# Four small edits to the order of work in a retention + two-MLP kernel: key scaling, weight sums, one held-back product, last stores

## The chip, the cores and the metric

The kernel runs on one core of a Trainium2 chip. The metric is the device time of one execution in microseconds (us). Before the change the median of three runs is 852.21 us (852.18 to 854.21).

## What is computed

Inputs are q, k and v (4 batches, 8 heads, 576 positions, 64 channels) and four weight matrices. In numpy terms:

```python
ret = scale * (q @ k.T) * Dmat          # Dmat: gamma ** distance below the diagonal, 0 above
x = (ret @ v)                           # 2304 tokens x 512
x = softplus(x @ w_in) @ w_out          # first MLP, 512 -> 2048 -> 512
out = (h * sigmoid(1.702 * h)) @ w2_out # second MLP, h = x @ w2_in
```

## The kernel before

Every factor of a large matrix product is split into a high and a low part (suffix h and l in the names), and a product is three matmuls: high by high, low by high, high by low. ACT casts the high part (`hi`, line 92) and DVE subtracts it to get the low part (`lo`, line 98). PE therefore has a long list of matmuls, and ACT and DVE prepare operands for it.

**Stages.** The tokens are cut into five blocks: the first 512 of each batch, and a short block "t" (256 columns) of the last 64 positions of all four batches. The order is batch 0, 1, 2, then "t", then batch 3 (line 297). Retention of batch 0 runs alone at the start (`first_batch`, line 556). Then the first MLP runs over the five blocks (`run_first`, line 213). Each block has 16 items f = 0 to 15: `mm1` makes 128 hidden features (tile ph, 12 matmuls), ACT applies softplus (tile g), `split` makes gh and gl, and `mm2` of the item two places back adds its share to the block's output (tile y, 12 matmuls). Then the second MLP runs (`run_second`, line 971) with a Strassen-like scheme of seven half-size products, so that its weights need sums and differences of their quarters.

**Work beside the first MLP.** While PE works on items, `side()` (line 685) is called four times an item. Each call adds a rate to two accumulators and advances two generators by one step for each whole unit:

- `side_gen` is the retention of the next batch (`batch`, line 538). A batch has eight pairs of heads-and-halves, and one pair takes three steps: `scale_pair` (line 364: ACT multiplies the pair's keys in place by decays, two instructions at line 373), then the pair's matmuls (`quad_step`, lines 463 and 502, into tile ps_so), then DVE's reading of that result (lines 510 to 533) and the load of the pair three places on (`load_pair`, line 353, DMA at line 356, on SP's queue, three buffers). A quad step also finishes the pair before it. Its first 16 matmuls use unscaled keys, the next need the scaled ones.
- `conv` is first the conversion of the first MLP's weights from 64-bit words (`convert_first`, line 113: ACT line 132, DVE lines 104, 105 and 110, ACT `hi`, DVE `lo`, tiles wa and w), then that of the second MLP's weights (`convert`), then the weight sums of the second MLP (`sums_steps`, line 746: four steps a unit, tiles sum and sum_halves). The sums run during block "t" at 0.66 step a call and during the last block at 0.7.

At a block's start, `pre` (line 1206) emits `split_block` (line 324): four ACT casts (tile xh) and four DVE subtractions (xl), each 128x512, and the block's first `mm1` reads them. Each engine executes its own instructions in the order in which they were emitted.

**Between the MLPs.** The first MLP's last three items still owe 36 products y (`pending`). The first two items of the second MLP (i = 0 and 1) work them off, 18 each, in five portions that stand ahead of places where PE must wait for ACT or DVE (`parts`, line 1034, taken by `fill`, line 1041): ahead of products 2 and 1, of product 6, of product 7, of products 4 and 5, and of product 3. All results of an item lie in halves X and Y of one PSUM bank (tile ph, line 1052).

**The end.** The second MLP's block "t" comes last (`second_layer_t`, line 919). It ends with two results y[0] and y[1], each one PSUM bank of 512 columns; y[0] is complete six matmuls before y[1]. `done_t` (line 1172) copies each to SBUF and stores it with two DMAs.

Of the kernel before, what the change touches and what calls it, by code (L numbers as in the profile page):

```python
# [16 lines left out]
T = 512  # L17
# [8 lines left out]
N2 = 256  # L26
# [7 lines left out]
def kernel(  # L34
# [36 lines left out]
    nc = tc.nc  # L71
# [4 lines left out]
    NF = w1_in.shape[0]  # L76
    KD = DM // P
    TAIL = S - T
# [13 lines left out]
    def hi(eng, dst, src):  # L92
        if eng == "a":
            nc.scalar.copy(dst, src)  # L94
        else:
            nc.vector.tensor_copy(dst, src)
# [197 lines left out]
    with tc.manual_schedule():  # L294
# [34 lines left out]
        def xf_tile():  # L329
            return xp.tile([P, KD, T], F32, tag="xf", name="xf")  # L330

        with ExitStack() as consts, ExitStack() as right, ExitStack() as second:
# [20 lines left out]
            def load_pair(i, tile_of=None, end_of=None):  # L353
                b, c, p = pairs[i]
                t = tile_of or ap.tile([P, KQV], F32, tag="raw", name="raw", bufs=RB)
                nc.sync.dma_start(out=t, in_=kqv[b, c, p])
                e = end_of
                if c and e is None:
                    e = ap.tile([P, ENDS], F32, tag="end", name="end", bufs=2)
                    nc.sync.dma_start(out=e, in_=ends[b, :, p])  # L360
                v = t[:, 2 * C0:].rearrange("p (t s d) -> p t s d", t=2, s=2)
                loaded[i] = t[:, 0:C0], t[:, C0:2 * C0], v[:, :, 0, :], v[:, :, 1, :], e

            def scale_pair(i, engines="aa", only="ap"):
                p, x = pairs[i][2], loaded[i][2]
                for h in range(2):
                    y, d = x[:, :, halves[h]], (sdec if i < 2 * NPAIR else sdec64)[:, 2 * p + h:2 * p + h + 1]
                    if engines[h] not in only:
                        continue
                    if engines[h] == "p":  # L370
                        nc.gpsimd.tensor_scalar(out=y, in0=y, scalar1=d, scalar2=None, op0=ALU.mult)
                    else:
                        nc.scalar.mul(y, y, d)
# [164 lines left out]
            def batch(b):  # L538

                xf[b] = xf_tile()  # L540
                i0, i1 = 2 * NPAIR * b, 2 * NPAIR * (b + 1)
                if b == 1:
                    for i in range(i0, i0 + RB):
                        load_pair(i)
                    yield
                for i in range(i0, i1 + 1):
                    if i < i1:
                        scale_pair(i)
                    yield
                    out_i = i - 1 if i > i0 else None  # L550
                    yield from quad_step(out_i, i if i < i1 else None)
                    if out_i is not None and out_i + RB < len(pairs):
                        load_pair(out_i + RB)
                    yield
# [77 lines left out]
            for _ in range(WARM):  # L632
# [3 lines left out]
                out=mask[:, 0:2, :].rearrange("p u j -> p (u j)"), in_=mask[:, 0:2, :].rearrange("p u j -> p (u j)"),  # L636
# [45 lines left out]
            conv = {"g": w1_gen, "acc": 0.0, "rate": 1.0}  # L682
# [236 lines left out]
            def second_layer_t(i):  # L919

                k, j = items[i]
                if j == 0:
                    sums_y[k] = [ps_y.tile([P, T], F32, tag="y", name="y") for _ in range(2)]
                for o in range(2):
                    gh, gl = g_operand(i, o)
                    for t in range(2):
                        c = slice(t * P, (t + 1) * P)
                        for n in range(2):
                            wh, wl = weight(i, "out", f"{o + 1}{n + 1}")
                            for z, (l, r) in enumerate(((gh, wh), (gl, wh), (gh, wl))):  # L930
                                seven([(l[:, c], r)], sums_y[k][t][:, n * N2:(n + 1) * N2],
                                      j == 0 and o == n == z == 0)
                                yield
                gs.pop(i)
# [36 lines left out]
            def run_second(pending):  # L971
# [52 lines left out]
                for i in range(n_items + 2):  # L1024
# [6 lines left out]
                    wino, post = cur is not None and not cur_t, prv is not None and not prv_t  # L1031

                    if i < 2:
                        more, parts = pending, ((4, 5, 3, 3, 3), (4, 5, 3, 3, 99))[i]
                    elif items[i - 2][0] == "t":
                        more, parts = second_layer_t(i - 2), (5, 3, 4, 4, 99)
                    else:
                        more, parts = second_layer(i - 2), (7, 10, 6, 7, 99)
                    parts = iter(parts)
# [14 lines left out]
                    if prv is not None:  # L1054
                        old = cs.pop(prv)
                        g = old["g"]
                        a = xp.tile([P, KD, T], F32R, tag="x8", name="ga", bufs=2)
                        a = a.rearrange("p (h k) (c n) -> p h (k c) n", h=2, c=2)
                        b = {}
                        gs[prv] = {"a": (a, ["11", "c3", "12", "22"] if post else [0, 1]), "b": b}  # L1060
                        if post:
# [4 lines left out]
                            c = {"c1": g[:, 4], "c2": g[:, 5], "c3": g[:, 1], "c4": g[:, 6]}  # L1066
# [104 lines left out]

            def done_t(e, y):
                yb = tp.tile([P, T], F32, tag="yb", name="yb", bufs=3)
                hi("v" if e % 2 else "a", yb, y)
                for j in range(2):
                    t0 = (2 * e + j) * S + T
                    nc.sync.dma_start(out=out[t0:t0 + TAIL, :], in_=yb[j * TAIL:(j + 1) * TAIL])

            n_full = NP * (len(order2) - 1)

# [25 lines left out]
            def pre(key, n, f):  # L1206
                i = order.index(key)
                if f == 0:
                    for _ in side_gen["g"]:
                        pass  # L1210
                    if i:
                        split_block(key, 1, xt if key == "t" else xf[key])
                        if turning:
                            turning.clear()
                            next(w2_gen, None)
                    if i + 1 < B:
                        side_gen["g"] = batch(i + 1)
                    else:
                        side_gen["g"] = iter(())
                    if key == "t":  # L1220
                        for _ in w2_gen:
                            pass
                        right.close()
                        cp = right.enter_context(tc.tile_pool(name="cp", bufs=2, side="right"))
                        sums_gen["g"] = sums_steps(cp)
                        conv.update(g=sums_gen["g"], rate=0.66)
                    if i + 1 == len(order):
                        conv["rate"] = 0.7
                        x2_load(order2[0])
                if i == 0:  # L1230
                    for n in range(0 if f else -1, 1):
                        w1_load(2 * (f + n) + 10, 2 * (f + n) + 11)
                    w1_need(f, 0)
                    w1_need(f - 2, 1)
                    counts[:] = STEPS[f] if f < len(STEPS) else ()
                    side_gen["rate"] = 0.62 if f >= 4 else 0.0
                    if f == NF - 2:
                        w2_read(0)
                        w2_read(1)
                    if f == NF - 1:  # L1240
                        for _ in w1_gen:
                            pass
                        next(w2_gen)
                        conv.update(g=w2_gen, acc=0.0, rate=1.0)
                elif i + 2 < len(order):
                    side_gen.update(acc=0.0 if f < 2 else side_gen["acc"], rate=0.52 if f else 0.0)
                    conv.update(acc=0.0, rate=1.0 if f or i == 2 else 0.0)
                if i < 2 and f == NF - 1:
                    turning.append(f)
                if i + 1 == len(order) and f >= 11:  # L1250
                    if f == 11:
                        for _ in sums_gen["g"]:
                            pass
                        right.close()
                        pool2["x"] = right.enter_context(tc.tile_pool(name="x2", bufs=1, side="right"))
                        consts.close()
                        pool2["g"] = second.enter_context(tc.tile_pool(name="g2", bufs=1))
                    if f == 12:
                        first_q.update(x_quarters(order2[0]))
                        for op in x_sums(order2[0], first_q):  # L1260
                            op()
                    if f >= 13:
                        names = [("21", "11"), ("c2", "c3"), ("c1", "c4", "22")][f - 13]
                        for late in [x_split(order2[0], nm, first_q[nm]) for nm in names]:
                            late()
# [83 lines left out]
```

## Time and profile before

| | |
|---|---|
| median of three runs | 852.21 us |
| the profiled execution | 852.78 us, of which the span from first to last instruction is 851.0 us |
| TensorE matmul (PE) busy | 834.7 us, 98% of the span |
| VectorE (DVE) busy | 568.7 us, 67% |
| ScalarE (ACT) busy | 405.3 us, 48% |
| mean granted TensorE clock | 0.997 of full speed |
| DMA | 217.70 MB, mean 256 GB/s |

PE rows are matmuls, PEld rows weight loads, and SPq rows DMA issues on SyncE's queue. In a timeline row the columns are start, duration, engine, line, operation, tiles written and read, shape and count; a bracket at the end is the idle time just before, with what ended it. The duration of a merged row (x12, say) runs from its first start to its last end. Matmul ends are modelled and overlap the next start: a 512-column matmul starts 0.227 us after the one before at full clock.

### The profile page before, as it was taken

The numbers are of one execution on the slowest core, as the hardware profiler recorded it, in microseconds if no ns is written. First come the engines' busy times: TensorE is split into PE (matmuls) and PEld (weight loads), VectorE is DVE, ScalarE is ACT, GpSimd is POOL, SyncE is SP. The second block draws the span as 40 slices with busy tenths as digits, with TensorE's granted clock in tenths as the row PEclk, the third lists the DMA queues.
The fourth block names the chain that finished last, engine by engine and source line by source line (L and its number), as shares of the span: only waits on it lengthen the run. The fifth ranks groups of instructions, "written<-read, shape, count | busy, mean of one in ns | idle before, by whom it ended". The sixth has DMA issues, their size and how long they took to land.

```text
span 851.0 us, 17585 instructions
## 1 busy us (share of the span) xinstructions
PE 834.7 (98%) x7115; PEld 751.4 (88%) x7115; DVE 568.7 (67%) x1158; ACT 405.3 (48%) x811; POOL 95.0 (11%) x178
## 2 busy tenths in 40 slices
PE   8989999999999999999999999999999999999997
PEld 5778888888888888997888899999999999999997
DVE  3998996666576764677434577787778777866621
ACT  4665545334453434455334555554555555554321
POOL 3200000211122111000000000100121011001000
PEclk9999999999999999999999999999999999999999
DMA  9966424898788874799996686977788779776611
GB/s 341 407 257 210 138 75 157 250 296 261 238 253 282 280 220 156 272 365 336 418 383 213 226 288 238 340 283 273 248 309 306 255 272 334 272 257 231 209 56 25
DMA packets 64481, 217.70 MB, mean 256 GB/s; under 512 B 6416, under 2 KB 21520, under 8 KB 52112
## 3 DMA queue, kind: packets, MB, share of 16 engines
q0 software_dynamic: 20704, 116.40, 39.8%
q1 hardware_dynamic: 43696, 100.17, 33.0%
q8 instruction: 56, 0.92, 0.4%
q14 instruction: 25, 0.20, 0.1%
HBM read 157.83 MB, written 58.72 MB: 254 GB/s over the span
## 4 chain that ended last, share of the span: by engine, by line
PE 85%; DVE 6%; DMA 4%; ACT 2%; issue 1%; SPq 0%; DVEq 0%; ACTq 0%
PE ph L878 20%; PE y L211 20%; PE ph L211 20%; PE m L878 18%; PE ps_so L463 3%; PE y L878 3%; DMA w_kqv<-kqv 1%; PE ps_so L502 1%; DMA odec<-outdecay 1%; DMA sums_in<-sum_halves 1%; DMA sums_out<-sum_halves 1%; DVE sum_halves L99 1%; DVE gl L99 0%; DMA whole<-whole_in 0%; DVE yb L950 0%
## 5 line engine op out<-in xcount | busy, mean ns | idle before, releaser
L211 PE MATMUL y<-gh,w 128*128 128x512 f32 (+1 forms) x640 | 197.3, 372 | 0.0
L211 PE MATMUL ph<-xh,w 128*128 128x512 f32 (+1 forms) x640 | 183.2, 371 | 2.3 <-ACT xh L94 2.3
L211 PEld LDWEIGHTS y<-gh,w 128*128 128x128 f32 x640 | 117.4, 189 | 21.0 <-issue 0.2
L211 PEld LDWEIGHTS ph<-xh,w 128*128 128x128 f32 x640 | 115.0, 189 | 23.0 <-ACT xh L94 2.9
L211 PE MATMUL y<-gl,w 128*128 128x512 f32 (+1 forms) x320 | 118.0, 369 | 0.0
L211 PE MATMUL ph<-xl,w 128*128 128x512 f32 (+1 forms) x320 | 118.0, 369 | 0.0
L878 PE MATMUL m<-w,ga 128*128 128x256 f32 x768 | 117.2, 282 | 0.5 <-DVE yb L950 0.5
L878 PE MATMUL ph<-xo_c,w 128*128 128x256 f32 x768 | 108.3, 283 | 0.0
L260 ACT ACTIVATE g<-ph 128x512 f32<-128x512 f32 (+1 forms) x80 | 44.2, 553 | 133.8 <-PE ph L211 131.1
L878 PE MATMUL ph<-xo,w 128*128 128x256 f32 x768 | 105.4, 282 | 0.5 <-DVE ho L1144 0.5
L99 DVE TENSOR_TENSOR gl<-g,gh 128x512 fp32r<-128x512 f32 (+1 forms) x80 | 50.8, 636 | 80.8 <-ACT gh L94 80.7
L878 PEld LDWEIGHTS m<-w,ga 128*128 128x128 f32 x768 | 102.8, 190 | 1.1 <-PE ph L878 1.1
L878 PEld LDWEIGHTS ph<-xo_c,w 128*128 128x128 f32 x768 | 97.9, 188 | 1.4 <-DVE he L1106 0.6
L878 PEld LDWEIGHTS ph<-xo,w 128*128 128x128 f32 x768 | 97.6, 189 | 1.5 <-DVE ho L1144 1.4
L878 PE MATMUL m<-w,gb 128*128 128x256 f32 x576 | 89.7, 282 | 0.0
L878 PEld LDWEIGHTS m<-w,gb 128*128 128x128 f32 x576 | 78.0, 191 | 0.0
L211 PEld LDWEIGHTS ph<-xl,w 128*128 128x128 f32 x320 | 60.3, 189 | 10.8 <-DVE xl L99 0.6
L211 PEld LDWEIGHTS y<-gl,w 128*128 128x128 f32 x320 | 60.5, 189 | 9.2
L99 DVE TENSOR_TENSOR ga<-g,ga 128x512 fp32r<-128x512 f32 x72 | 47.0, 685 | 9.1 <-ACT ga L94 9.1
L94 ACT CAST ga<-g 128x512 fp32r<-128x512 f32 x72 | 44.7, 621 | 15.3 <-PE y L878 7.9
L94 ACT CAST gh<-g 128x512 fp32r<-128x512 f32 (+1 forms) x80 | 46.3, 578 | 2.4
L99 DVE TENSOR_TENSOR gb<-g,gb 128x256 fp32r<-128x256 f32 x96 | 37.0, 419 | 13.8 <-ACT gb L94 13.8
(146 smaller groups left out, 1062.3 us busy)
## 6 DMA issues: line engine op xcount, KB each, us to landing
w<-sums_in POOLq DMA_DIRECT2D x32, 1024.0 KB, 5.5
w<-sums_out POOLq DMA_DIRECT2D x32, 1024.0 KB, 7.4
raw<-kqv SPq DMA_DIRECT2D x24, 512.0 KB, 4.7
w<-kept POOLq DMA_DIRECT2D x12, 1024.0 KB, 8.4
w_raw<-w_in SPq DMA_DIRECT2D x16, 512.0 KB, 9.6
w_raw<-w_out SPq DMA_DIRECT2D x16, 512.0 KB, 9.9
raw<-w_in POOLq DMA_DIRECT2D x16, 512.0 KB, 5.5
raw<-w_out POOLq DMA_DIRECT2D x16, 512.0 KB, 5.5
```

Source lines behind the costliest of these rows:

```text
L94: nc.scalar.copy(dst, src)
L99: nc.vector.tensor_tensor(out=dst, in0=src, in1=f32(h), op=ALU.subtract)
L211: nc.tensor.matmul(out_ap, l, r, start=first and i == 0, stop=last and i == k - 1)
L260: nc.scalar.activation(g, ph, AF.Softplus)
L463: nc.tensor.matmul(z[halves[half], t, at:at + D], l[halves[row]], rhs[halves[row]], start=(t, half) not in seen, stop=True, skip_group_che ...
L502: nc.tensor.matmul(z[n:n + D // 2, t, to:to + D], s[halves[h], m:m + D // 2], x[halves[h]], start=False, stop=True, skip_group_check=True)
L878: nc.tensor.matmul(out_ap, l, r, start=clear, stop=True, skip_group_check=True)
```

## The change

`batch` scales the first pair ahead of its loop, and from then on pair i+1 in the same step as pair i's matmuls, just ahead of them; the step that held only the scaling is now empty. `parts` of items 0 and 1 move one of the 18 products from the second portion to the last. The conversion rate is set to 0 at the last item of block "t", and for the last block it is 0.75 and not 0.7. `done_t` copies both results with DVE, the second one in two halves of 256 columns, and issues one store of each result on SP's queue and the other on ACT's.

```diff
@@ batch
+                scale_pair(i0)
                 for i in range(i0, i1 + 1):
-                    if i < i1:
-                        scale_pair(i)
                     yield
                     out_i = i - 1 if i > i0 else None
+                    if i + 1 < i1:
+                        scale_pair(i + 1)
                     yield from quad_step(out_i, i if i < i1 else None)
@@ run_second
-                        more, parts = pending, ((4, 5, 3, 3, 3), (4, 5, 3, 3, 99))[i]
+                        more, parts = pending, ((4, 4, 3, 3, 4), (4, 4, 3, 3, 99))[i]
@@ done_t
-                hi("v" if e % 2 else "a", yb, y)
-                for j in range(2):
+                for n in range(1 + e):
+                    c = slice(n * N2, (n + 1) * N2) if e else slice(0, T)
+                    hi("v", yb[:, c], y[:, c])
+                for j, queue in enumerate((nc.sync, nc.scalar)):
                     t0 = (2 * e + j) * S + T
-                    nc.sync.dma_start(out=out[t0:t0 + TAIL, :], in_=yb[j * TAIL:(j + 1) * TAIL])
+                    queue.dma_start(out=out[t0:t0 + TAIL, :], in_=yb[j * TAIL:(j + 1) * TAIL])
@@ pre
-                        conv["rate"] = 0.7
+                        conv["rate"] = 0.75
@@ pre
+                if key == "t" and f == NF - 1:
+                    conv["rate"] = 0.0
```

## Rows read from the trace of the kernel before

**Rows 1.** The profile page, busy time of each engine over the span.

```profile
PE 834.7 (98%) x7115; PEld 751.4 (88%) x7115; DVE 568.7 (67%) x1158; ACT 405.3 (48%) x811; POOL 95.0 (11%) x178
```

**Rows 2.** Waits of PE: us in total, times, longest.

```profile
PE ps_so L463 <- ACT raw L373: 2.4, 1, 2.4
PE ph L211 <- ACT xh L94: 2.3, 2, 1.7
```

**Rows 3.** Busy time by stretch, just after the longest wait of PE.

```profile
63.66:66.00 2.34, 2.34 (x56) 2.00 (x57) 2.34 (x3) 2.09 (x4) 0.00 (x0) 0.52 0.00 0
```

**Rows 4.** Timeline, ACT and PE around the second pair of batch 1.

```profile
53.77 1.15 ACT L132 ACTIVATE wa<-w_raw 128x1024 f32<-128x1024 f32 x1 [1.35 <-DVE w L99]
...
60.84 0.46 PE L463 MATMUL ps_so<-raw 64*64 64x64 f32 x16
...
62.25 1.04 ACT L94 CAST w<-wa 128x1024 fp32r<-128x1024 f32 x1 [3.89 <-DVE wa L110]
...
63.21 0.69 ACT L373 ACTIVATE raw<-raw,dec 128x128 f32<-128x128 f32 x2
```

**Rows 5.** The chain that ended last, in order of time: start, us, what.

```profile
69.57 2.72 PE ph L211 x12
...
82.35 1.08 PE ps_so L463 x56
...
83.78 2.95 PE ph L211 x12
...
89.45 1.36 PE ph L211 x6
...
272.13 1.08 PE ps_so L463 x56
```

**Rows 6.** Timeline, DVE: low parts of two weight pairs.

```profile
64.00 1.22 DVE L99 TENSOR_TENSOR w<-wa,w 128x1024 fp32r<-128x1024 f32 x1
...
87.72 1.22 DVE L99 TENSOR_TENSOR w<-wa,w 128x1024 fp32r<-128x1024 f32 x1
```

**Rows 7.** Waits from 42 to 130 us: DVE for a quad step's end.

```profile
DVE a L510 <- PE ps_so L502: 4.1, 4, 1.8
```

**Rows 8.** DMA issues from 265 to 266 us: KB each, us to landing.

```profile
raw<-kqv SPq DMA_DIRECT2D x1, 512.0 KB, 7.0
```

**Rows 9.** Line 356 from 40 to 330 us, the pairs' loads: time to landing.

```profile
DMA to landing us min/median/max: 3.5/4.6/10.2
```

**Rows 10.** Waits over the whole span: ACT's softplus for PE.

```profile
ACT g L260 <- PE ph L211: 131.1, 50, 4.5
```

**Rows 11.** Timeline, from block "t" to the last block.

```profile
383.93 1.29 ACT L94 CAST sum_halves<-sum 128x512 fp32r<-128x512 f32 x2 [0.51 <-DVE sum L739]
...
385.12 2.18 ACT L94 CAST xh<-xf 128x512 fp32r<-128x512 f32 x4
...
385.78 0.73 PE L211 MATMUL ph<-xh,w 128*128 128x512 f32 x2 [1.65 <-ACT xh L94]
386.51 0.50 PE L211 MATMUL ph<-xl,w 128*128 128x512 f32 x1
```

**Rows 12.** Timeline, item 0 of the second MLP, around products 6 and 3.

```profile
469.72 0.42 DVE L1106 TENSOR_TENSOR he<-ph,m 128x256 f32<-128x256 f32 x1 [0.99 <-ACT m L1092]
...
475.71 0.98 PE L878 MATMUL ph<-xo,w 128*128 128x256 f32 x6 [0.23 <-DVE ho L1144]
```

**Rows 13.** Timeline, item 1: products 2 and 1, and ACT's copy of Y.

```profile
477.45 1.60 PE L878 MATMUL ph<-xo,w 128*128 128x256 f32 x12
...
479.09 0.37 ACT L1092 COPY m<-ph 128x256 f32<-128x256 f32 x1 [0.69 <-PE ph L878]
```

**Rows 14.** Timeline, the last copy.

```profile
845.69 0.69 DVE L96 COPY yb<-y 128x512 f32<-128x512 f32 x1 [4.41 <-PE y L878]
```

**Rows 15.** Line 1177, the last stores: duration ns min/median/max, starts, time to landing.

```profile
L1177 SPq DMA_DIRECT2D out<-yb x4: 528/570/594, 845.6 to 847.4; - x4
...
DMA to landing us min/median/max: 2.3/2.3/2.4
```

## The prediction

> **What bounds the kernel.** I read the busy line first: PE is busy 98% of the span [rows 1], so time can come only from the few places where PE stands still or runs slowly. The list of waits says where. It has two entries that this change touches: 2.4 us, once, for ACT's scaling of keys, and 2.3 us for ACT's casts xh at a block's start [rows 2]. Next I read the granted clock by stretch. It is full nearly everywhere, but in the 2.34 us right after the first wait it is 0.52, that is mostly the 1.2 GHz level [rows 3]: PE stood still before it fell. So the first wait costs more than its own length. Then the timeline around both waits and around the end, to see who was late, and the chain of waits for the price of an undisturbed step.
>
> **Part A, the scaling a step ahead.** The late instruction is the scaling of batch 1's second pair: ACT runs it at 63.21 because the cast ahead of it in ACT's order waited 3.89 us for DVE until 62.25; PE had started that pair's matmuls at 60.84 and stopped after 16 [rows 4]. After the change this scaling is emitted just ahead of the first pair's matmuls. In ACT's order that is in front of the instruction that starts at 53.77 after 1.35 us of idle time [rows 4]; the two scalings take 0.69 us, so they fit into that gap and delay nothing. Done by 53.8, they are 7 us early. The third pair's scaling takes the old place, and is needed only at the next pair.
>
> What it is worth: from the pair's first matmul at 60.84 to the next ph run at 69.57 lie 8.73 us, made of the quad step and 12 products. The same work for a like pair goes from 82.35 to 83.78 + 2.95 = 86.73, 4.38 us [rows 5]. The difference is 4.35 us: the wait of 2.36 and about 2.0 of slow clock and restart. It counts only if PE does not run into the next late operand. Two weight tiles are close. The low part needed by the ph run at 69.57 is ready at 64.00 + 1.22 = 65.22 [rows 6]; PE would now come at 65.22 and needs it with the second matmul, 0.23 later: just in time, since DVE works without a break there and depends on no part of the stall. The one needed at 89.45 is ready at 88.94 [rows 5, 6], so with the second-matmul allowance 0.74 us early; PE would ask for it 4.35 sooner, so DVE must come 3.6 sooner. It can, because DVE itself lost 4.1 us in four waits for the end of quad steps [rows 7], and those ends move with PE. Not all four lie ahead of this tile, so I charge 0.2. Part A gives **4.15**. Bounds: 2.4 if the slow clock has another cause, 4.4 if nothing is charged. I take the upper side, because the clock is down nowhere else in PE's work.
>
> The Trainium skill, "TensorE: Matmul & The Clock Gate", in the section on the HAM clock gate, says that the throttled clock is the default state and that the activity of PE releases it. The row alone doesn't tell whether the slow stretch belongs to the wait or to the small matmuls that run in it; by the rule it belongs to the wait, and without it part A would be 2.4 and the sum 1.75 less.
>
> The other 20 scalings that move (seven in each of three batches are ahead by a step) end no wait of PE now, so they give nothing. They cost no instruction. What they add is exposure: ACT now asks for a pair's keys one step sooner, and the load is on SP's queue. The load issued in 265 to 266 us took 7.0 us to land [rows 8], at 272 to 273, and ACT will reach its scaling at about 272.1, beside that quad step [rows 5]. That is a wait of up to 1 us on ACT. Behind it in ACT's queue are the next g and gh; ACT idled 131.1 us over the 50 times that it waited for PE before g, 2.6 us each [rows 10], which hides it. Zero.
>
> **Part B, the sums rest.** At the turn to the last block ACT is free at 383.93 - 0.51 = 383.42, waits for a sum, casts two sum_halves, and starts xh only at 385.12; PE waits 1.65 us and begins at 385.78, then stops a little for xl until 386.51 [rows 11]. With rate 0 in that item these casts and the DVE sums beside them are not there. xh can start at 383.42; one cast is about 0.6, so PE starts at 384.07 and not at 385.78. DVE then needs 0.69 for xl: 384.05 to 384.75, and PE passes that point at 384.8 and not at 386.51. **1.7 us**. Bounds: 1.0 if an earlier sum's cast or DMA still sits in front, 2.1 if xl is also in time. The clock costs nothing here, as it stayed at full. The three steps put off move into the last block, where 0.75 for 0.7 over 44 calls makes up 2.2 of them; the sums still end at the same item, and ACT and DVE have room there. Zero.
>
> **Part C, the moved product.** In item 0, product 6 may not overwrite the bank before DVE's he ends at 469.72 + 0.42 = 470.14. That moment depends on ACT, not on the portion; with four products PE waits 0.23 longer there. Product 3 waits for ho, idle 0.23 [rows 12], and the fifth portion's extra product fills that. Both moments are fixed by ACT and DVE, so the sum is zero. Bounds: a loss of 0.2 per item, a gain of 0.2.
>
> **Part D, the end.** Now the last copy ends at 845.69 + 0.69 = 846.38 [rows 14]. Splitting it helps only if the first half can be copied while PE writes the second half of the same bank. It can't: in item 1, ACT's copy of Y, whose matmuls are the first 6 of 12, starts at 479.09, only after the last matmul into X ends at 477.45 + 1.60 = 479.05 [rows 13]. The Trainium skill, "PSUM — Partial Sum Buffer", in the section on bank collisions, says that TensorE and another engine must not use one bank at the same time; by it the split cannot start early, and the trace agrees; without it the last copy would end 0.4 sooner. So two copies of 0.42 (a 128x256 read from PSUM, as he in [rows 12]) follow one another: 845.69 to 846.53, 0.15 later than now. DVE's copy of y[0] takes the place of ACT's and is done before. The gain is in the queue: four issues of 0.53 to 0.59 on SP, the last at 847.4, landing 2.3 to 2.4 us after its issue [rows 15]. With two queues both last stores are issued at about 846.53, 0.9 earlier. No row shows an issue on ACT's queue; the nearest is SP's, from nothing extra to twice 0.57. **0.9 us** gained, bounds 0.3 to 1.1. Nothing stands behind these issues on ACT.
>
> **The sum.** 4.15 + 1.7 + 0 + 0.9 = 6.75. The profiled execution took 852.78, so 846.0; it stood 0.57 above the median, which gives **845.4** (0.8% less). By the bounds: least gain 2.4 + 1.0 - 0.4 + 0.3 = 3.3, most 4.4 + 2.1 + 0.4 + 1.1 = 8.0, so 848.9 to 844.2.
>
> **Rivals.**
>
> - *DVE becomes the bound in block 0.* Part A is half given back as waits for w at the two tight tiles. For it: zero spare at the first, and 3.6 us that DVE must catch up at the second. Against: its 4.1 us of waits for PE. Price 2.1: 847.5.
> - *The turn to the last block still waits*, for an earlier sum's cast that hangs on a store, or because xl is late. Part B gives 0.3: 846.8.
> - *Part A does not do what it says*: the stall is only moved, to whatever PE needs next. Gain 1.7 + 0.9: 849.6, on the edge of no change.
> - *Slower: ACT blocks on the loads.* The place is the new scaling in ACT's queue. It decides when a load lands more than about 7 us (the distance from issue to the new place) plus 2.6 us of headroom after its issue, in most pairs. The longest landing is 10.2, the median 4.6 [rows 9]. If all 21 landed at 10.2, PE would lose 0.6 at each, 12.6 in all: 858. The median speaks against it.
>
> **How the numbers follow.** A difference under 0.3% (2.6 us) can't be told from none. Forecast 0.62, DVE as the bound 0.16, a late turn 0.07 (all three faster: 0.85), part A moved 0.09 (about no change), ACT blocked 0.06 (slower). The range takes in the first three and the bounds, with 0.2 to 0.3 for the spread of medians: 844.0 to 849.2. It leaves out the last two, 0.15.
>
> **What would show it.** Right: no wait of PE for L373, no stretch of half clock near 63 us, PE's wait for xh under 0.3, and two stores each on SP and ACT with the last issue near the end of DVE's copy. Wrong: a new wait of PE for w, or for gh behind a wait of ACT for raw<-kqv, a dip of the clock elsewhere, or ACT's stores issued later than SP's.

## The result, and the profile after

The changed kernel takes 846.44 us (median of six runs, 845.58 to 847.27) against 853.12 for the kernel before in the same comparison (six runs, 852.13 to 854.86). The ratio is 0.9919, with a 95% interval of 0.9904 to 0.9934: 0.8% faster, 6.9 us. The forecast of 845.4 is 1.0 us below, and the range holds the time. The profiled execution took 845.58 us with a span of 843.9; [rows 1] has its busy line before. The page after:

```profile
PE 832.4 (99%) x7114; PEld 749.8 (89%) x7115; DVE 569.3 (67%) x1160; ACT 404.9 (48%) x810; POOL 95.0 (11%) x178
```

Nearly the same instructions and the same busy time, in a span that is 7.2 us shorter: the change took idle time and slow time out of PE's row, not work. Of the two entries of [rows 2], the list of PE's waits keeps the first of these lines; the other two are new (us in total, times, longest):

```profile
PE ph L211 <- ACT xh L94: 0.6, 1, 0.6
...
PE ph L879 <- DMA xo<-x: 0.2, 1, 0.2
PE ph L879 <- DVE he L1107: 0.2, 1, 0.2
```

The wait for ACT's scaling is gone, and of the two waits for xh the longer one. The stretch that answers to [rows 3], by windows (busy time of PE, PEld, DVE, ACT, POOL with counts, then granted clock, DMA share, GB/s): the whole quad step of the second pair, and the 2.86 us behind it.

```profile
59.69:61.12 1.43, 1.43 (x73) 1.27 (x72) 1.43 (x3) 0.00 (x0) 0.00 (x0) 1.00 0.00 0
61.12:63.98 2.86, 2.86 (x19) 2.36 (x13) 2.83 (x3) 2.75 (x5) 0.00 (x0) 1.00 0.42 142
```

The clock is 1.00 in both, the 2.4 GHz level, where it was 0.52 before. The timeline that answers to [rows 4 and 6] says why:

```profile
50.61 1.27 ACT L373 ACTIVATE raw<-raw,dec 128x128 f32<-128x128 f32 x4
52.66 1.16 ACT L132 ACTIVATE wa<-w_raw 128x1024 f32<-128x1024 f32 x1 [0.77 <-DVE w L99]
...
61.15 1.05 ACT L94 CAST w<-wa 128x1024 fp32r<-128x1024 f32 x1 [3.89 <-DVE wa L110]
62.10 0.69 ACT L373 ACTIVATE raw<-raw,dec 128x128 f32<-128x128 f32 x2
...
82.98 1.22 DVE L99 TENSOR_TENSOR w<-wa,w 128x1024 fp32r<-128x1024 f32 x1
...
83.96 0.79 PE L211 MATMUL ph<-xh,w 128*128 128x512 f32 x2
84.59 0.39 PE L211 MATMUL ph<-xl,w 128*128 128x512 f32 x1
```

Four scalings, those of the first two pairs, run at 50.61, and the instruction behind them still had 0.77 us of idle time. ACT's cast waits the same 3.89 us for DVE as before, and the scaling behind it comes at 62.10, but it is now the third pair's, which nobody needs yet. The last three rows show the price: DVE's low part ends at 82.98 + 1.22 = 84.20, PE has been in that ph run since 83.96, and its third matmul starts 0.63 us after the first. In the kernel before, the same two starts lie 0.46 apart (89.29 and 89.75). So 0.17 us are given back there, and 0.07 at the tile of the ph run that begins at 63.98, where the same distance is 0.53. The turn to the last block, against [rows 11]:

```profile
377.52 0.41 ACT L94 CAST gh<-g 128x256 fp32r<-128x256 f32 x1
377.83 2.18 ACT L94 CAST xh<-xf 128x512 fp32r<-128x512 f32 x4
...
378.71 0.28 PE L211 MATMUL y<-gh,w 128*128 128x256 f32 x1
...
378.83 0.63 PE L211 MATMUL ph<-xh,w 128*128 128x512 f32 x2
...
381.81 1.29 ACT L94 CAST sum_halves<-sum 128x512 fp32r<-128x512 f32 x2 [1.80 <-DVE sum L740]
```

The casts xh follow directly on the item's gh, PE goes from the last product into the new block without a bracket, and the sums' casts come 4 us later, beside PE's work. Last the end, against [rows 14, 15]: the timeline, and the two lines on the stores (duration ns min/median/max, first and last start).

```profile
838.28 1.47 DVE L96 COPY yb<-y 128x512 f32<-128x512 f32 x3 [3.69 <-PE y L879]
839.00 1.27 SPq L1180 DMA_DIRECT2D out<-yb  x2
839.00 1.44 ACTq L1180 DMA_DIRECT2D out<-yb  x2
```

```profile
L1180 SPq DMA_DIRECT2D out<-yb x2: 488/508/529, 839.0 to 839.8; - x2
L1180 ACTq DMA_DIRECT2D out<-yb x2: 560/608/657, 839.0 to 839.8; - x2
```

**Where the 7.2 us came from.** Five moments can be found in the trace of each kernel and cut its span into six stretches: the first matmul of the second pair's quad step (60.84 in [rows 4]), the second matmul of the next ph run, which is the first there to need the low part of w (69.6 before), the first matmul of the last block (385.78 in [rows 11]), the first product of the second MLP, and the end of the last matmul. The stretches in us, read off the twelve timelines (the eleven names below "before" are the changed kernel and the experiments):

```
                   up to    quad step  to last   last     second   tail    span
                   the pair +12 prod.  block     block    MLP
before               60.84     8.80    316.15     81.67    378.19    5.39  851.03
after                59.69     4.52    314.63     81.35    378.77    4.91  843.87
no_scale_ahead       59.59     8.77    314.34     81.27    378.25    4.94  847.18
scale_ahead_only     60.42     4.52    316.40     81.69    378.22    5.38  846.63
no_sums_rest         60.65     4.52    317.32     81.71    378.22    4.95  847.38
old_end              61.19     4.52    314.59     81.35    378.24    5.37  845.27
stall_filled         60.89     7.43    316.04     81.65    379.90    5.37  851.28
load_step_later      60.80     4.52    314.65     81.31    378.32    4.94  844.54
no_moved_product     60.73     4.52    314.61     81.27    378.27    4.94  844.34
end_by_halves        60.52     4.52    314.64     81.65    379.02   14.81  855.16
act_queue_end        59.96     4.52    314.60     81.47    378.22    5.55  844.33
whole_copy           61.10     4.52    315.34     81.53    378.22    4.98  845.70
```

Before to after: 1.15 in the opening, 4.28 at the quad step, 1.52 up to the last block, 0.32 in the last block itself, 0.48 in the tail, and 0.58 lost in the second MLP; together 7.17. The opening and the second MLP are not the change's: the instructions there are the same in all twelve kernels apart from the moved product and the earlier scaling, and over the twelve profiles the opening takes from 59.59 to 61.19 and the second MLP from 378.19 to 379.90 without following any edit. In the changed kernel 0.5 of the 0.58 is one more wait, for a load of xo at 622.30 (the 0.2 of the wait list and the restart behind it); the six kernels at 378.2 to 378.3 that have the product moved do not have it. That leaves 4.28 + 1.52 + 0.32 + 0.48 = 6.6 for the change.

### The profile page after: what moved, and what is told of

Read it like the earlier page. It is cut to its first block, busy times and chain, and to the rows that moved or that the text cites. A ratio compares the mean times of both kernels' runs of the same rounds, so it can differ in the third digit from the quotient of the medians.

```text
span 843.9 us, 17587 instructions
## 1 busy us (share of the span) xinstructions
PE 832.4 (99%) x7114; PEld 749.8 (89%) x7115; DVE 569.3 (67%) x1160; ACT 404.9 (48%) x810; POOL 95.0 (11%) x178
## 4 chain that ended last, share of the span: by engine, by line
PE 85%; issue 7%; DMA 3%; DVE 3%; POOL 1%; ACT 1%; SPq 0%; POOLq 0%; DVEq 0%; ACTq 0%
PE ph L211 24%; PE y L211 23%; PE ph L879 16%; PE m L879 14%; PE ps_so L463 3%; PE y L879 3%; DMA xo<-x 1%; DMA w_kqv<-kqv 1%; PE ps_so L502 1%; POOL w L798 1%; DMA w_raw<-w_in 1%; DVE yb L951 0%; DVE ga L99 0%; DVE gb L99 0%; DVE g L1098 0%
## 5 line engine op out<-in xcount | busy, mean ns | idle before, releaser
L260 ACT ACTIVATE g<-ph 128x512 f32<-128x512 f32 (+1 forms) x80 | 44.1, 551 | 110.3 <-PE ph L211 106.4
```

Source lines behind the costliest of these rows:

```text
L260: nc.scalar.activation(g, ph, AF.Softplus)
```

## The experiments

The theory to be tested was that of the forecast: A, the scaling a step ahead, is worth a wait and a stretch of slow clock, some 4.2 us; B, the rest of the sums, 1.7 to 2; C, the moved product, nothing; D, the end, under 1. The rivals: the slow clock belongs to the small matmuls and not to the wait; ACT's earlier demand for keys costs time; the end is limited by something other than the queue of SP.

**The parts undone, one at a time.** `no_scale_ahead` is the changed kernel with the old loop:

```diff
-                scale_pair(i0)
                 for i in range(i0, i1 + 1):
+                    if i < i1:
+                        scale_pair(i)
                     yield
                     out_i = i - 1 if i > i0 else None
-                    if i + 1 < i1:
-                        scale_pair(i + 1)
```

> The changed kernel with the old place of the key scaling (part A undone). If part A is worth what the prediction says, PE stands still again for 2.3 to 2.4 us at the second pair of batch 1, the granted clock falls to about half behind it, and the kernel is about 4.2 us slower than the changed one: near 850.5 us, ratio to before about 0.997. If the 7 us came from elsewhere (the opening, the turn), the wait shows but PE has caught up a few items later, and the ratio stays near 0.993.

Measured: 851.13 us (seven runs), ratio 0.9968 (0.9955 to 0.9981). The gain shrinks from 0.81% to 0.32%, so part A carries 0.49% of 853, 4.2 us (give or take 1.7, an estimate from the two intervals). Wait and slow stretch are both back (the wait list, then the window behind it):

```profile
PE ps_so L463 <- ACT raw L373: 2.4, 1, 2.4
```

```profile
62.45:64.75 2.30, 2.30 (x56) 2.00 (x56) 2.30 (x3) 2.04 (x4) 0.00 (x0) 0.51 0.00 0
```

The quad step's stretch is 8.77 again, and the one to the last block is 314.34, 0.3 shorter than with part A: the place where DVE's weight tile is late is no longer reached early.

`scale_ahead_only` is the opposite, the kernel before with this loop alone changed (the diff above read backwards).

> The kernel before with part A alone. Theory: PE gains 4.2 us at that pair and keeps 4.0 of it to the end, ratio about 0.995 (848.9 if before is at 853). Rival, DVE as the bound: PE waits for w at the tiles of the ph runs that began at 69.57 and 89.45 before, 2 us are given back, ratio about 0.9975.

Measured: 848.44 (four runs), ratio 0.9941 (0.9921 to 0.9961), 5.0 us with an interval from 3.3 to 6.7. In the trace the quad step's stretch falls from 8.80 to 4.52, and the way to the last block grows from 316.15 to 316.40. So part A by itself is worth 4.28 - 0.25 = 4.0 in the profiles, and its work at the other 20 pairs gives nothing more. By the stretches and by both timings A does not need B, C or D.

`no_sums_rest` leaves out part B:

```diff
-                        conv["rate"] = 0.75
+                        conv["rate"] = 0.7
...
-                if key == "t" and f == NF - 1:
-                    conv["rate"] = 0.0
```

> The changed kernel with rates 0.66 and 0.7 as before (part B undone). Theory: the two casts of sum_halves stand ahead of xh again, PE waits 1.6 to 1.9 us at the turn to the last block, and the kernel is 1.7 to 2.0 us slower than the changed one. Rival: the gain at the turn was only given to PE's next wait, and the end moves by under 0.5.

Measured: 848.66 (four runs), ratio 0.9939 (0.9920 to 0.9958). That is 0.2% from the changed kernel, or 1.7 us, but the two intervals overlap; the trace has to carry this one. Timeline at the turn:

```profile
380.63 1.29 ACT L94 CAST sum_halves<-sum 128x512 fp32r<-128x512 f32 x2 [0.51 <-DVE sum L740]
381.83 2.18 ACT L94 CAST xh<-xf 128x512 fp32r<-128x512 f32 x4
...
382.49 0.73 PE L211 MATMUL ph<-xh,w 128*128 128x512 f32 x2 [1.52 <-ACT xh L94]
```

The picture of [rows 11] is back: two casts of sums in front of xh, and PE waits 1.52 us. The stretch to the last block is 317.32 against 314.63, 2.7 longer, more than part B can be. PE's wait list shows what the rest is:

```profile
PE ph L211 <- ACT xh L94: 2.1, 2, 1.5
...
PE ph L211 <- ACT g L260: 0.8, 1, 0.8
```

The second line is inside block "t": there ACT had stood 4.03 us before a cast that starts at 372.56, for a store of an earlier sum (sums_out<-sum_halves), and the g behind it came late. The other kernels with the old rate, before, `scale_ahead_only` and `stall_filled`, do not show this wait, and `whole_copy`, whose edit is at the very end, does (0.5 us, and a stretch of 315.34). So I put it down to the execution and not to the edit; it was not repeated. From start to start of the matmuls it takes 1.0 (the 0.8 of the list and the restart). Without it the edit costs 2.7 - 1.0 = 1.7 at the turn and 81.71 - 81.35 = 0.4 behind it.

`no_moved_product` puts the product of part C back:

```diff
-                        more, parts = pending, ((4, 4, 3, 3, 4), (4, 4, 3, 3, 99))[i]
+                        more, parts = pending, ((4, 5, 3, 3, 3), (4, 5, 3, 3, 99))[i]
```

> The changed kernel with the old portions (part C undone). Forecast: the wait ahead of product 6 is 0.2 shorter and the one ahead of product 3 is 0.2 longer, in both items, and everything behind item 1 stands where it stood: 0.0, at most 0.2 either way. If the moved product fills a true gap, everything behind item 0 is 0.2 later, and behind item 1 0.4.

Measured: one execution, 846.04. The second MLP takes 378.27 us, as it does in six kernels that have the product moved (378.22 to 378.32; the other two, the changed kernel and `end_by_halves`, have the wait for xo more). What moves is a bracket. First the changed kernel, then this one, at the places ahead of product 6 and product 3:

```profile
462.33 0.39 PE L211 MATMUL y<-gl,w 128*128 128x512 f32 x1
462.93 0.98 PE L879 MATMUL ph<-xo_c,w 128*128 128x256 f32 x6 [0.21 <-DVE he L1107]
...
468.43 0.74 PE L879 MATMUL ph<-xo,w 128*128 128x256 f32 x4
```

```profile
463.88 0.99 PE L879 MATMUL ph<-xo_c,w 128*128 128x256 f32 x6
...
469.38 0.87 PE L879 MATMUL ph<-xo,w 128*128 128x256 f32 x5 [0.23 <-DVE ho L1145]
```

The 0.21 us that PE now waits for he are the 0.23 that it no longer waits for ho.

`old_end` puts the old `done_t` back:

```diff
-                for n in range(1 + e):
-                    c = slice(n * N2, (n + 1) * N2) if e else slice(0, T)
-                    hi("v", yb[:, c], y[:, c])
-                for j, queue in enumerate((nc.sync, nc.scalar)):
+                hi("v" if e % 2 else "a", yb, y)
+                for j in range(2):
...
-                    queue.dma_start(out=out[t0:t0 + TAIL, :], in_=yb[j * TAIL:(j + 1) * TAIL])
+                    nc.sync.dma_start(out=out[t0:t0 + TAIL, :], in_=yb[j * TAIL:(j + 1) * TAIL])
```

> The changed kernel with the old last copies and four stores on SP (part D undone). By the prediction's price it is 0.9 us slower, by the first trace of the changed kernel only 0.45 (from the last matmul's end to the span's end 5.4 us as before and not 4.9), since the last store on ACT's queue took 2.8 us to land and the one on SP 2.3. If landings on ACT vary by chance, this difference is between 0.4 and 1.0.

Measured: 847.14 (four runs), ratio 0.9927 (0.9906 to 0.9949), too near to 0.9919 to tell apart by time. The tail, from the last matmul's end to the span's end, tells it: 5.37 with the old end, 4.91 to 4.98 in every kernel with copies by DVE and two queues. Part D is worth 0.45, half of the forecast.

**Why the end gave half.** Two kernels take its halves apart. `act_queue_end` issues all four stores on ACT's queue, `whole_copy` copies y[1] in one piece:

```diff
-                for j, queue in enumerate((nc.sync, nc.scalar)):
+                for j, queue in enumerate((nc.scalar, nc.scalar)):
```

```diff
-                for n in range(1 + e):
-                    c = slice(n * N2, (n + 1) * N2) if e else slice(0, T)
-                    hi("v", yb[:, c], y[:, c])
+                hi("v", yb, y)
```

> The changed kernel with all four last stores on ACT's queue. If that queue is the slower one by itself, each store lands 2.7 to 2.9 us after its issue also with nothing on SP's queue, and the span ends about 0.5 us later after the last matmul than with SP alone (5.4): 5.8 to 6.0. If the 2.8 us come from two stores of one moment sharing the engines, the stores, now one after the other, land in 2.3 to 2.4 and the span ends at 5.4.

> The changed kernel with y[1] copied by one DVE instruction of 512 columns. If no half can be copied while PE writes its bank, the copy ends 0.69 to 0.73 us after the last matmul and not 0.79, and the span's end follows by 0.06. If the split let DVE start early, the end is 0.2 to 0.4 later.

Measured: one execution each, 846.34 and 847.49. The issues with the time to landing, in the changed kernel, with ACT's queue alone, and with SP's alone (`old_end`); the columns are tiles, queue, count, KB each, median us from issue to landing:

```profile
out<-yb SPq DMA_DIRECT2D x2, 128.0 KB, 2.3
out<-yb ACTq DMA_DIRECT2D x2, 128.0 KB, 2.8
```

```profile
out<-yb ACTq DMA_DIRECT2D x4, 128.0 KB, 2.3
```

```profile
out<-yb SPq DMA_DIRECT2D x4, 128.0 KB, 2.3
```

ACT's queue alone lands a store as fast as SP's alone. Only where two stores are issued at the same moment does one take 2.7 to 2.9 (2.69 to 2.94 over the six kernels that do it), and it is always ACT's. The packets say where the time goes. All packets under way in the changed kernel until 840.79, 1.79 us after the first issue on each queue, are on SP's queue (q1; ACT's is q10; packets, MB, share of the 16 engines):

```profile
q1 hardware_dynamic: 60, 0.12, 32.7%
```

Over the six kernels the first packet of ACT's store starts 1.73 to 1.81 us after its issue, that of SP's 1.18 to 1.42; with one queue alone it is 1.18 to 1.27 on either. Once begun, ACT's store moves its data in 0.52 to 0.77 us, no slower than with one queue (0.71 to 0.80). So the loss is a later start and not a slower transfer; what holds the start back stays open. The Trainium skill, "DMA: Bandwidth & Descriptors", in the section "Issuing engines are not separate DMA queues", says that DMAs started by different engines run on the same 16 DMA engines and interleave, so that several issuers only save the time of issuing. The trace agrees as far as nothing but issuing is saved, and less of it is left: the last issue is 0.97 earlier, and 0.44 of that is lost again before the landing. Four issues on one queue cost a tail of 5.55 on ACT's and 5.37 on SP's. Most of that difference stands ahead of the stores: the first issue comes 0.12 later on ACT's, because DVE's copy of y[0] takes 0.69 us and ACT's in `old_end` 0.59. An issue takes 0.56 to 0.61 us on ACT and 0.53 to 0.59 on SP.

`whole_copy` has a tail of 4.98 against 4.91. DVE's two halves end 0.46 and 0.79 us after the last matmul, one whole copy 0.73 after it. The split makes the copies end 0.06 later, and the span does not follow, since ACT's last store lands 2.94 us after its issue with the whole copy and 2.81 with the split one. The split brings nothing of note, because the first half too starts only 0.04 us behind the last matmul, although the last three matmuls write the second half alone. Both halves lie in one bank, and in the trace only the last matmul into it sends the signal for which the copy waits; whether the bank or the place of the signal holds the copy back was not separated.

**An end that should have been better.** If each half is stored as soon as it is copied, in both batches' rows with one issue, only one issue stands behind the last copy. `end_by_halves`:

```diff
+                rows = out.rearrange("(b s) n -> b s n", s=S)[2 * e:2 * e + 2, T:, :]
                 for n in range(1 + e):
...
-                for j, queue in enumerate((nc.sync, nc.scalar)):
-                    t0 = (2 * e + j) * S + T
-                    queue.dma_start(out=out[t0:t0 + TAIL, :], in_=yb[j * TAIL:(j + 1) * TAIL])
+                    (nc.sync if e == n else nc.scalar).dma_start(out=rows[:, :, c], in_=yb[:, c])
```

> The changed kernel with three last stores and not four: y[0] whole on SP, then the two column halves of y[1], the first on ACT's queue as soon as its copy ends, the second on SP. The last issue is on SP at the end of the last copy, where the changed kernel has one there and one on ACT. If ACT's queue is the slower one to land (2.8 against 2.3 us), the span ends 0.4 to 0.5 us sooner after the last matmul than in the changed kernel; if it was chance, they are equal. Rows of 1 KB and not 2 KB could cost some tenths.

Measured: 856.31 (twelve runs), ratio 1.0036 (1.0022 to 1.0051), 10 us slower than the changed kernel. The forecast for this run was wrong. All of it lies in the tail, 14.81 us. First the issues, then the window in which nothing but these stores is under way (no engine has an instruction in it):

```profile
840.39 1.33 SPq L1179 DMA_DIRECT2D out<-yb  x2
840.85 1.13 ACTq L1179 DMA_DIRECT2D out<-yb  x1
```

```profile
843.00:852.00 9.00, 0.00 (x0) 0.00 (x0) 0.00 (x0) 0.00 (x0) 0.00 (x0) 0.53 0.13 47
```

The second number from the right is the mean busy share of the 16 DMA engines: 0.13 is two of them (2/16 = 0.125). The shorter rows of 1 KB are not the cause: the share is the same while only the store of y[0] is under way, whose rows have 2 KB as before:

```profile
841.60:845.60 4.00, 0.00 (x0) 0.00 (x0) 0.00 (x0) 0.00 (x0) 0.00 (x0) 0.75 0.13 34
```

The store's outermost dimension is the batch, of size 2; the stores that it replaces have 64 rows outermost. The Trainium skill, same page, in the section "Why a DMA increments its semaphore by 16 and not by 1", says that the number of engines is the largest up to 16 that divides the size of the slowest dimension of both sides. That would make two here, and the trace agrees with its 0.13; that the outermost dimension decides was not tried with another size.

**Is the slow clock the wait's or the small matmuls'?** `stall_filled` is the kernel before, with ten matmuls of 512 columns, whose result nobody reads, in the place where PE stood waiting for the scaling. PE still cannot go on sooner, but it does not stand still:

```diff
+                    if i == 2 * NPAIR + 1:
+                        busy = bank(ps_h, "h")
+                        xh = xs[1, 0][0]
+                        for _ in range(10):
+                            nc.tensor.matmul(busy, xh[:, 0, 0:P], xh[:, 1, :], start=True, stop=True)
```

> The kernel before, with ten more matmuls of 512 columns (2.27 us of work into a bank that nobody reads) between the 16 matmuls on unscaled keys and the ones that wait for the scaling. PE is as late as before, but not idle. If the slow clock belongs to PE's standing still, the stretch of half clock is gone, the quad step and the 12 products behind it run at full clock, and the end comes 1.7 to 2.0 us sooner than before. If it belongs to the quad step's small matmuls, the clock falls as before and the time is that of before.

Measured: 852.12 (ten runs), ratio 0.9984 (0.9967 to 1.0000). The window that answers to [rows 3]:

```profile
63.78:66.00 2.22, 2.22 (x60) 1.89 (x60) 2.22 (x3) 1.97 (x4) 0.00 (x0) 1.00 0.00 0
```

The clock is 1.00 there. The stretch is 7.43, against 8.80 with the wait and 4.52 without it. So at this place 1.4 of the 4.3 us belong to the clock, and they go when PE doesn't stand still: the small matmuls are not the cause. The rest comes apart at the pair's 17th matmul, the first that needs the scaled keys. It starts 0.28 us after the pair's first matmul in the changed kernel, 2.82 before, 2.89 with the filling. From there to the end of the stretch PE takes 4.24, 5.98 and 4.54. So the 4.28 are 2.54 of waiting (2.36 in the list), 1.44 of slow clock and 0.30 of restart at full clock. The Trainium skill, "TensorE: Matmul & The Clock Gate", in the section on the HAM clock gate, says that activity of PE releases the throttle; this pair of windows, 0.52 and 1.00, agrees.

The timed gain, 0.16% or 1.4 us with an interval from 0 to 2.8, is what the slow clock cost; the 1.7 to 2.0 that were expected had the restart in them. The profiled execution, 852.98 us, is no shorter than that of before for another reason, 520 us later: PE waits once more for ho, 1.37 us ahead of 586.73, behind a DVE instruction that itself stood 2.82 us for a store of x_lo, and the second MLP takes 379.90. Whether that comes in every execution of this kernel is not known.

**Would ACT block on the loads?** `load_step_later` issues each pair's load one step later than the changed kernel does, so that the load has a step less, a third of a pair's time, until ACT needs it:

```diff
                     yield from quad_step(out_i, i if i < i1 else None)
+                    yield
                     if out_i is not None and out_i + RB < len(pairs):
                         load_pair(out_i + RB)
-                    yield
```

> The changed kernel with each pair's load issued one step (about a third of a pair's period, some 3 us) later, so that ACT meets its scaling before the keys have landed. ACT should wait 2 to 4 us for raw<-kqv at most pairs of the three batches. If the headroom of ACT hides such waits, PE shows no wait for it and the time is that of the changed kernel. By the rival of the prediction, each wait beyond the headroom comes back on PE: some tenths at each of up to 21 pairs, 3 to 12 us in all.

Measured: 848.23 (four runs), ratio 0.9933 (0.9908 to 0.9959); the interval holds the changed kernel's 0.9919. ACT's wait list:

```profile
ACT g L260 <- PE ph L211: 64.9, 31, 4.2
...
ACT raw L373 <- DMA raw<-kqv: 23.5, 8, 4.8
```

ACT now does wait for the loads, 23.5 us in eight times (not at most of the pairs, as expected), up to 4.8. PE shows no wait behind it, and the way to the last block is 314.65, the same as the changed kernel's 314.63. What shrinks is ACT's idle time before g: 106.4 us in 43 waits in the changed kernel, 64.9 in 31 here. The rival's place is real, and in this execution the headroom covers it, up to 4.8 us. It is the fastest of the four (846.24; the others took 847.43 to 849.23), and the interval would also hold a cost of some 3 us, so for the others this is not shown. In the changed kernel itself ACT waits for a load once, for 0.4 us.

## Why the prediction was right

**Part A: 4.15 forecast, 4.0 to 4.2 measured.** The step that carried it was the comparison of [rows 5], a quad step and 12 products with and without the stall: 4.35 there, 4.28 in the trace after. Its starts come partly from the chain and partly from the timeline, which differ by up to 0.16 us; by the starts of the matmuls alone the same rows of before give (69.41 - 60.84) - (86.57 - 82.28) = 4.28, and both tight tiles are 0.16 tighter than it had them. The choice of the upper side was right: the slow clock belongs to PE's standing still, as `stall_filled` shows. The 2.0 of slow clock and restart were 1.74, and the wait was 0.18 longer from start to start than the list's 2.36, so the two parts were a little off and their sum was not. The charge of 0.2 for the weight tile was right as well: 0.17 at that tile, 0.07 at the one before, 0.25 to 0.3 over the whole stretch. That DVE can catch up because its own waits for quad steps move with PE is seen in the wait list of 42 to 130 us, where [rows 7] had 4.1:

```profile
DVE a L510 <- PE ps_so L502: 1.0, 2, 0.6
```

**Part B: 1.7 forecast, about 2 measured.** PE's wait of 1.65 went entirely, as worked out (1.7). The bound of 2.1 supposed that xl is also in time, and it nearly was: the third matmul of the new block starts 0.47 us after the first (378.83 to 379.30) and not 0.73. So a further 0.3 went behind the turn, and the forecast, which let PE pass that point 1.7 earlier, was 0.3 low. That part is in some measure luck: xh starts 1.00 us ahead of the block's first matmul here (377.83 and 378.83), but 0.70 ahead in `end_by_halves`, where xl is late again and the last block takes 81.65. In `act_queue_end` and `whole_copy` some of it stays as well (81.47 and 81.53). The sums put off cost nothing that a stretch shows.

**Part C: 0 forecast, 0 measured,** with the two waits of 0.2 exchanged at the places that were named.

**Part D: 0.9 forecast, 0.45 measured.** This is the one term that was mis-sized. The step that failed is that stores on two queues land after their issue like the stores on SP's queue. The last issue did come 0.97 earlier: 0.83 us after the last matmul's end (839.79 less 838.96) and not 1.80 (847.45 less 845.65). But of two stores issued at one moment ACT's begins to move 0.4 to 0.6 us after SP's and lands in 2.7 to 2.9 instead of 2.3 to 2.4. That the split copies can't start early held (0.04 us behind the last matmul), though the runs show when and not why; that they cost 0.15 did not (0.06).

**The sum.** 4.0 + 2.0 + 0 + 0.45 = 6.5 by stretches (6.6 from the table above), 6.9 by the ratio, 6.75 forecast. The errors of B and D, 0.3 up and 0.45 down, nearly cancel, which is luck. Of the 1.0 us by which the forecast of the time is low, 0.9 lie in the level from which it was taken: the median of before was 852.21 over the three runs that were known and 853.12 over six.

**The rivals.** DVE as the bound of block 0: two places just in time, as said, but 0.17 given back and not 2.1. A late turn: not seen in the changed kernel. Part A only moved: refuted, since the stretch is 4.52 in every kernel with part A and no more than 0.3 of the gain is given back up to the last block (316.40 against 316.15). ACT blocked on loads: the mechanism exists, and its cover holds in the profiled execution of `load_step_later`.

## What to carry to other kernels

Price a stall of the bounding engine by the distance between two like pieces of work on either side of it, not by the wait that the list names: here 2.4 us of waiting cost 4.3, and the granted clock behind the wait accounts for 1.4 of the difference. Before moving an operand's preparation one step ahead, look at what else in that engine's queue becomes earlier (its loads) and at how long the engine idles in front of the next thing that others wait for; that idle time is the cover. At a kernel's end, count landing as well as issue: of the 1.0 us that a second queue saved in issuing here, 0.4 went before the second store's data moved, and a store with a short outermost dimension can cost more than all the rest of the end.

## What was not expected of the hardware

Two 128 KB stores issued at the same moment on SP and ACT do not land alike: SP's in 2.30 and 2.37 us, ACT's in 2.70 and 2.81, while ACT's queue alone needs 2.32 to 2.40. ACT's packets begin 0.4 to 0.6 us after SP's. Why it is ACT's that comes second stays open.

A store whose outermost dimension is 2 kept 0.13 of the DMA engines busy and made the tail 10 us longer.

The slow clock of the kernel before is not the same in each execution. Of its 23 runs on one chip, three show a mean granted clock of 0.999 and take 850.3 us on average, nine show 0.997 and take 852.7, three show 0.995 and take 855.4. This mean also counts the tail, where PE has nothing left: in the profiled execution the clock is 0.50 from 848.8 to the end, which takes 0.001 off the mean, while the slow stretch behind the wait takes 0.002. `end_by_halves`, with no slow stretch in front of its long tail, shows 0.992 to 0.994. So a step of 0.001 says little, but the three runs at 0.999 cannot hold the whole slow stretch. All six runs of the changed kernel lie at 0.999 or 1.000. The seven runs of `no_scale_ahead` spread from 0.995 to 1.000 too, with less order in their times (849.79 at 1.000, 848.88 at 0.996). So what part A removes differs between executions, and it may be more than the profiled one shows, which would fit the 5.0 that `scale_ahead_only` was timed at; its interval doesn't settle that.
